# Shifting the SBUF tiles of a block-attention and two-MLP kernel to other byte addresses

## The chip, the cores and the metric

The kernel runs on one core of one Trainium2 chip. The metric is the device time of one execution in microseconds (us). The median of three runs of the kernel before is 985.55 us (985.31 to 985.72).

## The reference

The kernel computes an attention with a block-causal mask (blocks of 64 positions, 4 batches, 8 heads, 576 positions, head width 64) and feeds its 2,304 tokens of width 512 through two MLPs with a hidden width of 2,048. All arrays are float32.

```
scores = q @ k.T / sqrt(64); scores = where(block_i >= block_j, scores, -1e9)
x = softmax(scores) @ v                 # 2304 tokens x 512
h = x @ w1_in;  g = h * cos(h);         y = g @ w1_out
h = y @ w2_in;  g = max(h, 0) ** 2;   out = g @ w2_out
```

## The kernel before, in words

**Recording and order.** The body does not issue instructions at once: a `Recorder` notes every operation with its engine, its cost and what it reads and writes, a list scheduler (`schedule`) puts all operations in one order with its own cost figures, and `issue` emits them in that order. A tile gets its real buffer only when its first operation is emitted (`VTile.alloc`). The order doesn't depend on addresses.

**Precision.** Each float32 operand of the MLPs is split in a high and a low part (`hi_part`, `lo_part`), held as `fp32r`, and each product becomes three matmuls (`mm3`, all issued at L548): high by high and high by low with the same stationary operand, low by high with another. For every two matmuls that read a high operand on the split side there is thus one that reads the low part.

**The work by time.** Some 400 us are attention, mixed with the first halves of both products of the first MLP: `h_banks` multiplies the weights `w` (stationary, 128x128) by the tokens `xs1` or `xs2` (moving, 256 or 320 columns), `out_T` multiplies `w` (stationary) by the activations `g` (moving, 256 or 320 columns). What is left of the MLPs comes in three stages of five rounds (`ROUNDS`). In each, `quad` or `two` multiply weight parts `w` (stationary) by token parts `x0` to `x6` (moving, 256 columns) into `h` banks, and a second product makes `y`: in the first stage `out_T` with 512 moving columns of `g` (256 in the short round), in the second `g` stationary and `w` moving with 512 columns, in the third `out_quad`, `g` stationary and `w` moving with 256 columns. There the moving parts lie in buffers of several tags: two in `raw`, two in `x`, one in `so`, nine in `w` (`right_factors`), and the stationary ones in `ws`, `t`, `c`, `n`, `t0` to `t3` and the `g` tiles (`g_forms`).

**Memory.** A pool allocates its tiles one behind the other, and each takes a multiple of 32 bytes of every partition. Pools on the left are stacked upwards in the order in which they are opened: `const`, `wa` (16 weight tiles of 4,096 bytes), `cv` (`raw`, `t`, `c`), `st` (`so`, `ws`), `g`, `o`, then `xs1` and `tmp1`, in whose place `tmp3` opens later. Those on the right are stacked downwards: `att`, in whose place `wo` (7 weight tiles) and then `x3` (`x`, `x0` to `x6`) open later. `transition` (L607) closes the old pools and opens the new ones. Every large tile is a multiple of 128 bytes, but for `raw` (1,026 words, 4,128 bytes with padding), so that all tiles of a pool share one residue. Worked out from the declarations, and the first weight tile begins at byte 2,272:

| tiles | byte address modulo 128, before |
|---|---|
| `w` in `wa` and in `wo` | 96 |
| `raw`, first and second buffer | 96 and 0 |
| `t`, `c`, `so`, `ws`, `g`, `o`, `xs1`, `xs2`, tiles of `tmp1` and `tmp3` | 32 |
| `x`, `x0` to `x6`, and all large tiles of attention | 96 |
| `ident` and `zeros` | 0 and 64 |

Slices that the matmuls read start at multiples of 128 bytes within their tile, so an operand has its tile's residue.

**Warm-up.** At the start TensorE multiplies a tile `zeros` (bf16, 256 columns) by itself 40 times (kind "warm"), between the first transposes.

Of the kernel before, what the change touches and what calls it, by code (L numbers as in the profile page):

```python
# [10 lines left out]
F32 = mybir.dt.float32  # L11
F32R = mybir.dt.float32r
BF16 = mybir.dt.bfloat16
I32 = mybir.dt.int32
# [16 lines left out]
RAWS = 2  # L31
# [345 lines left out]
def real(v):  # L377
    return v.ap() if isinstance(v, View) else v
# [3 lines left out]
def kernel(  # L382
# [28 lines left out]
    def of(kind):  # L411
        def wrap(fn):
            def run(*args, **kw):
                with R.of(kind):
                    return fn(*args, **kw)

            return run

        return wrap
# [4 lines left out]
    def act(out, in_, func, bias=None, scale=None, accum_out=None, after=()):  # L424
        kw = {}
        n = sum(x is not None and not isinstance(x, float) for x in (bias, scale))
        if accum_out is not None:
            n += 1
        cost = out.size / 1.2 + (50 if psum(in_) else 92) + 93 * n + (49 if out.size == 512 and func == ACTF.Relu and bias is not None else 0) + (115 if out.halves != 3 else 0)

        def fn():
            kw = {a: real(x) for a, x in (("bias", bias), ("scale", scale), ("accum_out", accum_out)) if x is not None}
            return nc.scalar.activation(real(out), real(in_), func, **kw)  # L433

        return R.op("ACT", cost, fn, [x for x in (out, accum_out) if x is not None], [in_, bias, scale], after)
# [10 lines left out]
    def stt(out, a, s, b, op0, op1):  # L446
        dve(
            out.size / 0.96 + 68,
            lambda: nc.vector.scalar_tensor_tensor(real(out), real(a), s, real(b), op0=op0, op1=op1),  # L449
            [out], [a, b], int(not psum(a) and not psum(b)),  # L450
        )
# [5 lines left out]
    def flexible(kind, alts, w, r):  # L457
        R.any([alts[e] for e in FREE[kind].split()], w, r)
# [112 lines left out]
    def dma(out, in_, size, service=None):  # L571
        R.op(
            "DMA", max(400.0, size / 360.0), lambda: nc.sync.dma_start(out=real(out), in_=real(in_)), [out], [in_],
            lat=1250,
        ).service = size / 420.0 if service is None else service
# [20 lines left out]
    def opened(stack, *names, **kw):  # L596
        got = []
        for n in names:
            p = Pool(n, **kw)
            p.open(stack)  # L600
            got.append(p)
        return got

    def later(names, **kw):
        return [Pool(n, **kw) for n in names]

    def transition(closes, stack, opens, old):  # L607

        def fn():
            closes()  # L610
            for p in opens:
                p.open(stack if p.stack is None else p.stack)

        users = {o for o in R.ops if any(t.pool in old for t in o.tiles)}
        o = R.op("HOST", 0.0, fn, after=users)
        for p in opens:
            p.after = (o,)
        return o

    s1, att = ExitStack(), ExitStack()  # L620
    (dram,) = opened(ctx, "dram", space=DRAM)
    const, wa_p, cv, st_p, g_p, o_p = opened(ctx, "const", "wa", "cv", "st", "g", "o")
    (psum_p,) = opened(ctx, "ps", space=PSUM)
    banks = Banks(8, *BANKS)
    xs_p, tmp = opened(s1, "xs1", "tmp1")
# [2 lines left out]
    def T(pool, shape, dtype, tag, bufs=1):  # L628
        return R.tile(pool, shape, dtype, tag, bufs, whole=pool.kw.get("space") == PSUM)
# [68 lines left out]
    @of("weights")  # L698
    def weight_part(src, hi, lo):

        w = weight_piece(src)
        hi_part(hi, w)
        lo_part(lo, w, hi)

    @of("weights")
    def weight_piece(src, gate=()):

        w = T(cv, [128, 512], F32, "c", 3)
        if not wide:
            dma(w, src, 128 * 2048)  # L710
        else:


            raw = T(cv, [128, 1026], I32, "raw", RAWS)
            R.op(
                "DMA", 128 * 4096 / 360.0,
                lambda: nc.sync.dma_start(out=real(raw).bitcast(U8)[:, 1:4097], in_=src.bitcast(U8)), [raw], after=gate, lat=1250,
            ).service = 2400.0
            mid = View(raw, [lambda a: a[:, 1:1025].rearrange("p (n t) -> p n t", t=2)[:, :, 0]], np.arange(512), 3)
            top = View(  # L720
                raw, [lambda a: a[:, 2:1026].bitcast(I8).rearrange("p (n t) -> p n t", t=8)[:, :, 0]],
                np.arange(512), 3,
            )
            t = T(cv, [128, 512], I32, "t", 2)


            wi = w.bitcast(I32)
            act(t, top, ACTF.Relu, bias=minus56, scale=2.0**27)
            act(wi, top, ACTF.Relu, bias=minus56, scale=-2.0**27)
            flexible(  # L730
                "wt",
                {
                    "DVE": (
                        "DVE", 512 / 0.96 + 68,
                        lambda: nc.vector.tensor_tensor(real(wi), real(t), real(wi), op=ALU.subtract), 1,  # L735
                    ),
                    "POOL": (
                        "POOL", 512 * 2.1 + 350,
                        lambda: nc.gpsimd.tensor_tensor(real(wi), real(t), real(wi), op=ALU.subtract), 1,
                    ),  # L740
                },
                [w], [t, w],
            )
            stt(wi, mid, 5, wi, ALU.logical_shift_right, ALU.bitwise_or)
        return w
# [64 lines left out]
    @of("later")  # L810
    def left_weights(w, c, to):

        gate = R.ops[-1:]
        for k in range(2):
            left_parts([weight_piece(w[i * 128:i * 128 + 128, c * 512:c * 512 + 512], gate) for i in (k, k + 2)], k, to)

    @of("later")
    def right_weights(w, c, to):

        gate = R.ops[-1:]  # L820
        for m in range(2):
            rows = [c * 512 + i * 128 for i in (m, m + 2)]
            right_parts_of([weight_piece(w[r:r + 128, :], gate) for r in rows], m, to)
# [388 lines left out]
    def new_g():  # L1212
        return [[T(g_p, [128, 2, 512], F32R, f"g{i}{m}") for m in range(HALF // 2)] for i in "hl"]
# [4 lines left out]
    def first_in(b, r):  # L1218
        g = new_g()
        in_cos(tmp, w1i, xs[b, r], g, GROUPS[r - 1][1], TOGETHER if (b, r) == (0, 1) else 1)  # L1220
        return g
# [31 lines left out]
    for group, steps in WORK:  # L1253
        R.phase = 0 if group == (0, 1) else 1 + group[0]
        g = first_in(*group)
        if group == (0, 1):
            w1o = weights(wa_p, row_chunks(w1_out, 0, 2))
        for i in steps:
            attend(i)
        if group in ((0, 2), (1, 1)):  # L1260
            c = group[0]
            left_weights(w1_in, 2 + c, wi_d[c])
        if group in ((1, 2), (2, 1)):
            c = group[0] - 1
            staged_weights(row_chunks(w1_out, 2 + c, 3 + c), wo_d[c:c + 1])
        if group == (3, 1):
            wo_p, x3_p = later(("wo", "x3"), side="right")
            transition(att.close, ctx, [wo_p, x3_p], (sb,)).hook = lambda: banks.own.update(s=0, t=0, a=0, y=2)
        if group == (3, 2):
            (tmp3,) = later(("tmp3",))  # L1270
            transition(s1.close, ctx, [tmp3], (xs_p, tmp))
            left = factors(wi_d[:2], 0)
        first_out(*group, g)
# [149 lines left out]
    def g_forms():  # L1423

        small = [(st_p, f"ws{i}", 1) for i in range(2)] + [(cv, "t", 2)] * 2 + [(cv, "c", 3)] * 3
        small += [(tmp3, "n", 1)] + [(tmp3, f"t{i}", 1) for i in range(4)]
        large = [(g_p, f"g{i}{m}", 1) for i in "hl" for m in range(HALF // 2)]
        got = [{}, {}]
        for c in range(2):
            for i in (0, 3, 4, 5, 6, 1, 2):  # L1430
                if small:
                    got[c][i] = [T(pool, [128, 2, 256], F32R, tag, n) for pool, tag, n in (small.pop(0), small.pop(0))]
                else:
                    pool, tag, n = large.pop(0)
                    t = T(pool, [128, 2, 2, 256], F32R, tag, n)
                    got[c][i] = [t[:, j] for j in range(2)]
        return got
# [86 lines left out]
    for stage in range(3):  # L1524
# [4 lines left out]
        for turn_, i in enumerate(ROUNDS[stage]):  # L1529
# [3 lines left out]
            if stage < 2:  # L1533
                xs = (load_quarters if i < 4 else load_plain)(src, c0, xp_d[i] if stage and turn_ < 4 else None)
                g = new_g()
            else:
                if turn_:
                    xs = kept_parts(xp_d[i], FIRST if i < 4 else (0, 1, 4))
                g = g_forms()
# [90 lines left out]
```

## Time and profile before

| | |
|---|---|
| median of three runs | 985.55 us |
| the profiled execution's own time | 983.81 us |
| its span, first to last instruction | 981.9 us |
| mean granted clock of TensorE | 0.997 |
| busy: PE, weight loads, DVE, ACT, POOL | 960.9, 866.3, 714.6, 602.0, 208.2 us |
| moved by DMA | 185.29 MB, 189 GB/s |

PE is TensorE's matmul side, PEld its weight loads, which overlap matmuls. The end of a matmul in the profile is modelled and lies past the start of the next one, so the mean duration of a matmul says little: what one costs in a dense row is read from start to start. The chain of waits does this: it goes back from the last instruction to what released each step, and a piece "0.98 PE h x9" says that nine matmuls took 0.98 us from the first one's start to the next piece.

### The profile page before, as it was taken

To read this page: it belongs to the slowest core of one execution; us is meant where nothing else is said; L and a number is where in the kernel's file an instruction comes from. 1 tells how busy PE (TensorE), PEld (TensorE's weight loads), DVE (VectorE), ACT (ScalarE), POOL (GpSimd) and SP (SyncE) were. 2 spreads that over 40 slices of the span, in tenths; PEclk is the share of its full clock that TensorE was granted. 3 is DMA by queue.
4 is the path that set the end of the run, shared out by engine and by line. 5 is a ranking of instruction groups with operands and counts; after the bars stand their busy time and mean duration, and the time that the engine had idled before them with its cause. 6 is when DMAs were issued, how large, how long until landed. Compare 5 with 4: busy or idle time off the path is not lost.

```text
span 981.9 us, 19283 instructions
## 1 busy us (share of the span) xinstructions
PE 960.9 (98%) x6996; PEld 866.3 (88%) x6996; DVE 714.6 (73%) x1581; ACT 602.0 (61%) x1285; POOL 208.2 (21%) x313
## 2 busy tenths in 40 slices
PE   7879999999999999999999999999999999999998
PEld 5657987888898989999989889998898999999998
DVE  6898677685877455696878887978785747749565
ACT  6787578786987774483858476758574433324222
POOL 3563234455787780000000000000000000000000
PEclk9999999999999999999999999999999999999999
DMA  7754132455566256643266899796947679525321
GB/s 192 194 151 124 48 99 74 103 169 170 176 201 190 88 169 256 244 176 107 87 193 193 326 359 321 264 345 205 343 139 235 239 259 401 198 88 194 100 68 59
DMA packets 155150, 185.29 MB, mean 189 GB/s; under 512 B 71728, under 2 KB 119856, under 8 KB 155056
## 3 DMA queue, kind: packets, MB, share of 16 engines
q1 hardware_dynamic: 155056, 184.07, 57.1%
q8 instruction: 55, 0.90, 0.4%
q14 instruction: 39, 0.32, 0.1%
HBM read 114.29 MB, written 69.73 MB: 187 GB/s over the span
## 4 chain that ended last, share of the span: by engine, by line
PE 87%; DMA 5%; DVE 4%; ACT 1%; POOL 1%; issue 1%; SPq 0%; DVEq 0%; POOLq 0%
PE y L548 37%; PE h L548 35%; PE t L566 6%; PE a L558 5%; PE s L558 4%; PE s L548 1%; DMA x<-xp_d 1%; DMA w<-wf_d 1%; DMA wi_d<-so 1%; DMA x<-x_d 1%; DVE e L1033 1%; DMA xp_d<-x 1%; DMA w<-wi_d 1%; DVE c L735 1%; DVE c L449 1%
## 5 line engine op out<-in xcount | busy, mean ns | idle before, releaser
L548 PE MATMUL h<-x,w 128*128 128x256 f32 x2304 | 326.3, 283 | 0.9 <-DMA x<-xp_d 0.5
L548 PEld LDWEIGHTS h<-x,w 128*128 128x128 f32 x2304 | 304.5, 191 | 5.4 <-DVE r L442 1.1
L548 PE MATMUL y<-gh,w 128*128 128x256 f32 (+2 forms) x832 | 215.9, 330 | 6.9 <-POOL w L467 6.6
L548 PEld LDWEIGHTS y<-gh,w 128*128 128x128 f32 x832 | 144.6, 189 | 19.0 <-POOL w L467 7.6
L548 PE MATMUL y<-gl,w 128*128 128x256 f32 (+2 forms) x416 | 135.4, 329 | 0.0
L548 PE MATMUL y<-w,gh 128*128 128x512 f32 (+1 forms) x450 | 124.2, 355 | 0.5 <-DVE gh L490 0.4
L548 PEld LDWEIGHTS y<-w,gh 128*128 128x128 f32 x450 | 79.3, 189 | 12.6 <-DVE gh L490 0.6
L433 ACT ACTIVATE e<-e,st 128x256 f32<-128x256 f32 (+4 forms) x144 | 82.8, 577 | 9.2 <-DVE st L1033 7.7
L1033 DVE CUSTOM_DVE_ANT_0 e<-s,mask 128x128 f32<-128x128 f32 (+4 forms) x160 | 71.3, 478 | 22.4 <-PE s L558 14.8
L531 POOL TENSOR_SCALAR e<-e,st 128x256 f32<-128x256 f32 (+4 forms) x116 | 72.7, 637 | 62.8 <-DVE st L1054 36.7
L548 PEld LDWEIGHTS y<-gl,w 128*128 128x128 f32 x416 | 78.6, 189 | 6.5 <-issue 0.8
L548 PE MATMUL y<-w,gl 128*128 128x256 f32 (+1 forms) x306 | 83.7, 334 | 0.0
L472 ACT ACTIVATE gh<-r 128x512 fp32r<-128x512 f32 (+1 forms) x85 | 51.3, 610 | 38.9 <-DVE r L1391 17.2
L566 PE MATMUL t<-ident,e 128*128 128x128 f32 (+1 forms) x400 | 64.4, 280 | 4.6 <-DVE e L535 2.1
L442 DVE TENSOR_TENSOR o<-y,o 128x512 f32<-128x512 f32 (+1 forms) x55 | 34.9, 636 | 44.4 <-PE y L548 43.6
L490 DVE TENSOR_TENSOR gl<-r,gh 128x512 fp32r<-128x512 f32 (+1 forms) x83 | 54.7, 664 | 16.4 <-ACT gh L472 13.6
L548 PE MATMUL h<-xs2h,w 128*128 128x320 f32 x256 | 62.0, 313 | 0.0
L566 PEld LDWEIGHTS t<-ident,e 128*128 128x128 f32 (+1 forms) x400 | 46.1, 141 | 13.3 <-POOL e L531 4.4
L501 ACT ACTIVATE r<-t 128x384 f32<-128x384 f32 (+1 forms) x95 | 49.0, 531 | 13.4 <-PE t L566 11.7
L433 ACT ACTIVATE t<-raw,minus 128x512 int32<-128x512 int8 x64 | 48.7, 760 | 13.8 <-DMA raw<-in_moe_w_out_dram 8.1
L548 PEld LDWEIGHTS y<-w,gl 128*128 128x128 f32 x306 | 50.4, 188 | 6.1
L548 PE MATMUL h<-xs1h,w 128*128 128x256 f32 x256 | 53.3, 289 | 1.8 <-POOL w L467 0.8
(172 smaller groups left out, 1835.5 us busy)
## 6 DMA issues: line engine op xcount, KB each, us to landing
wi_d<-so SPq DMA_DIRECT2D x84, 256.0 KB, 2.8
w<-wi_d SPq DMA_DIRECT2D x42, 512.0 KB, 6.7
raw<-in_moe_w_in_dram SPq DMA_DIRECT2D x32, 512.0 KB, 4.6
raw<-in_moe_w_out_dram SPq DMA_DIRECT2D x32, 512.0 KB, 4.2
xp_d<-x SPq DMA_DIRECT2D x24, 512.0 KB, 6.1
x<-xp_d SPq DMA_DIRECT2D x24, 512.0 KB, 5.5
y_d<-o SPq DMA_DIRECT2D x34, 256.0 KB, 2.4
o<-y_d SPq DMA_DIRECT2D x32, 256.0 KB, 4.0
```

Of the source, the lines that this page charges most:

```text
L433: return nc.scalar.activation(real(out), real(in_), func, **kw)
L442: out.size / 0.96 + 68, lambda: nc.vector.tensor_tensor(real(out), real(a), real(b), op=op), [out], [a, b],
L449: lambda: nc.vector.scalar_tensor_tensor(real(out), real(a), s, real(b), op0=op0, op1=op1),
L472: "ACT": ("ACT", n / 1.2 + 92, lambda: nc.scalar.activation(real(hi), real(x), ACTF.Copy)),
L490: lambda: nc.vector.tensor_tensor(real(lo), real(x), real(f(hi)), op=ALU.subtract), 1,
L501: "ACT": ("ACT", n / 1.2 + 50, lambda: nc.scalar.activation(real(out), real(ps), ACTF.Copy)),
L531: lambda: nc.gpsimd.tensor_scalar(real(out), real(x), real(s), 1.0, op0=ALU.mult, op1=ALU.mult),
L548: lambda: nc.tensor.matmul(real(ps), lhsT=real(lhsT), rhs=real(rhs), start=start, stop=stop, skip_group_check=True),
L558: nc.tensor.matmul(real(ps), lhsT=real(l), rhs=real(r), start=start, stop=stop, skip_group_check=True)
L566: lambda: nc.tensor.transpose(real(out), real(in_), real(ident)[0:rows, 0:rows]), [out], [in_, ident],
L735: lambda: nc.vector.tensor_tensor(real(wi), real(t), real(wi), op=ALU.subtract), 1,
L1033: lambda: nc.vector.tensor_tensor_reduce(out=real(e), in0=real(ps), in1=real(m), scale=-1.0, scalar=BIG, op0=ALU.add, op1=ALU.min, accum_o ...
```

## The change

Small tiles that nothing reads or writes (`shim1` to `shim4`) are put between pools, and `raw` grows from 1,026 to 1,056 words, of which the same 1,026 are used. No operation is added, removed or moved.

```diff
+    def shim(stack, name, n, **kw):
+
+        if n:
+            p = stack.enter_context(tc.tile_pool(name=name, bufs=1, **kw))
+            p.tile([128, n // 4], F32, tag=name, name=name)
+
     def transition(closes, stack, opens, old):
 
         def fn():
             closes()
-            for p in opens:
+            for i, p in enumerate(opens):
+                if i:
+                    shim(stack, "shim4", 64, side="right")
                 p.open(stack if p.stack is None else p.stack)
@@
-    const, wa_p, cv, st_p, g_p, o_p = opened(ctx, "const", "wa", "cv", "st", "g", "o")
+    (const,) = opened(ctx, "const")
+    shim(ctx, "shim1", 32)
+    (wa_p,) = opened(ctx, "wa")
+    shim(ctx, "shim2", 64)
+    cv, st_p, g_p, o_p = opened(ctx, "cv", "st", "g", "o")
+    shim(ctx, "shim3", 96, side="right")
@@
-            raw = T(cv, [128, 1026], I32, "raw", RAWS)
+            raw = T(cv, [128, 1056], I32, "raw", RAWS)
```

Worked out in the same way, the residues become these; the last two columns name the moving and the stationary operand's.

| product | before: moving, stationary | after: moving, stationary |
|---|---|---|
| `h` from `xs1`, `xs2` by `w` | 32, 96 | 64, 0 |
| `h` from `x0` to `x6` by `w` | 96, 96 | 64, 0 |
| `y` from `g` by `w` (first MLP) | 32, 96 | 64, 0 |
| `y` from `w` by `g` (second MLP, second stage) | 96, 32 | 0, 64 |
| `y`, third stage, `w` moving (9 of 14 parts) | 96, 32 | 0, 64 |
| `y`, third stage, `raw` and `x` moving (4 of 14) | 96 (one `raw`: 0), 32 | 64, 64 |
| `y`, third stage, `so` moving (1 of 14) | 32, 32 | 64, 64 |
| attention, among themselves | 96, 96 | 0, 0 |

## Rows read from the trace of the kernel before

**Rows 1.** The page, busy time by engine over the whole span.

```profile
PE 960.9 (98%) x6996; PEld 866.3 (88%) x6996; DVE 714.6 (73%) x1581; ACT 602.0 (61%) x1285; POOL 208.2 (21%) x313
```

**Rows 2.** Busy time by stretch: stretch, length, engines, granted clock, DMA share, GB/s.

```profile
core 0: us, PE busy (x) PEld busy (x) DVE busy (x) ACT busy (x) POOL busy (x), PEclk, DMA share, GB/s
0.00:100.00 100.00, 83.96 (x582) 62.77 (x584) 79.70 (x210) 75.58 (x184) 47.73 (x73) 0.97 0.63 165
...
500.00:600.00 100.00, 99.92 (x597) 88.41 (x596) 83.27 (x155) 67.62 (x127) 0.00 (x0) 1.00 0.82 286
600.00:700.00 100.00, 100.00 (x657) 91.12 (x656) 84.40 (x152) 65.64 (x119) 0.00 (x0) 1.00 0.82 292
```

**Rows 3.** The page, the chain that ended last, by engine and by line.

```profile
PE 87%; DMA 5%; DVE 4%; ACT 1%; POOL 1%; issue 1%; SPq 0%; DVEq 0%; POOLq 0%
PE y L548 37%; PE h L548 35%; PE t L566 6%; PE a L558 5%; PE s L558 4%; PE s L548 1%; DMA x<-xp_d 1%; DMA w<-wf_d 1%; DMA wi_d<-so 1%; DMA x<-x_d 1%; DVE e L1033 1%; DMA xp_d<-x 1%; DMA w<-wi_d 1%; DVE c L735 1%; DVE c L449 1%
```

**Rows 4.** The chain in order of time: start, us to the next piece, matmuls.

```profile
108.44 7.04 PE h L548 x48
...
271.56 7.46 PE h L548 x64
...
492.69 20.54 PE y L548 x88
...
843.93 11.52 PE h L548 x96
...
862.67 6.60 PE y L548 x56
```

**Rows 5.** Groups of MLP matmuls on PE, shapes apart: count, busy us, mean ns.

```profile
L548 PE MATMUL h<-x,w 128*128 128x256 f32 x2304 | 326.3, 283 | 0.9 <-DMA x<-xp_d 0.5 <-DVE r L442 0.4
L548 PE MATMUL y<-w,gh 128*128 128x512 f32 x288 | 92.0, 395 | 0.0
L548 PE MATMUL y<-gh,w 128*128 128x512 f32 x256 | 83.3, 396 | 0.0
L548 PE MATMUL y<-gh,w 128*128 128x256 f32 x320 | 70.7, 292 | 6.9 <-POOL w L467 6.6 <-DVE w L490 0.2
L548 PE MATMUL h<-xs2h,w 128*128 128x320 f32 x256 | 62.0, 313 | 0.0
L548 PE MATMUL y<-gh,w 128*128 128x320 f32 x256 | 61.9, 312 | 0.0
L548 PE MATMUL h<-xs1h,w 128*128 128x256 f32 x256 | 53.3, 289 | 1.8 <-POOL w L467 0.8 <-POOL xs1h L467 0.6 <-DVE w L490 0.3
```

**Rows 6.** The chain inside 4.66 to 5.55 us, the bf16 warm-up matmuls.

```profile
4.64 0.98 PE h L548 x9
```

**Rows 7.** PE in order of time near the end: start, us, instruction, count.

```profile
974.96 0.84 PE L548 MATMUL y<-w,t 128*128 128x256 f32 x6
975.64 0.84 PE L548 MATMUL y<-w,gl 128*128 128x256 f32 x6
```

**Rows 8.** PE in order of time, third stage, moving operand in the second `raw` buffer.

```profile
816.95 0.88 PE L548 MATMUL y<-raw,gh 128*128 128x256 f32 x6
817.66 0.88 PE L548 MATMUL y<-raw,ws 128*128 128x256 f32 x6
```

**Rows 9.** Two groups on DVE that differ in width alone.

```profile
L442 DVE TENSOR_TENSOR r<-h,p 128x512 f32<-128x512 f32 x48 | 33.0, 688 | 30.1 <-PE h L548 29.7 <-ACT gh L472 0.3
L442 DVE TENSOR_TENSOR r<-h,r 128x320 f32<-128x320 f32 x32 | 15.5, 489 | 8.1 <-ACT r L433 8.0
```

**Rows 10.** The chain in order of time, entry of the third stage.

```profile
802.10 6.00 DMA w<-wi_d
...
808.16 9.17 DMA w<-wf_d
...
817.40 10.54 DMA x<-xp_d
```

## The prediction

> **What bounds the kernel now.** I read the page's busy times first: TensorE's matmul side is busy for 98% of the span, the next engine, DVE, for 73% [rows 1]. The stretches show where that is not the whole story: in the first 100 us PE is busy for only 84 us, from 500 to 700 us for all of it, with DVE at 83 and 84 us of 100 and the DMA share at 0.82; the granted clock is 1.00 there, the upper level of 2.4 GHz [rows 2]. The chain that ended last runs 87% over PE, and 37 + 35 = 72% of the span, 707 us, over the MLP matmuls of L548 [rows 3]. So what one dense MLP matmul costs, start to start, decides.
>
> The chain in order of time gives that cost by width and by the residues of the two operands. 256 columns, moving and stationary operand both at 96: 11.52 us / 96 = 120.0 ns. 256 columns, 64 bytes apart: 6.60 / 56 = 117.9 ns in the third stage (nearly all pairs there), 7.46 / 64 = 116.6 ns from `xs1`. 320 columns, 64 apart: 7.04 / 48 = 146.7 ns. 512 columns, 64 apart: 20.54 / 88 = 233.4 ns [rows 4]. At 2.4 GHz and a column a cycle they would be 106.7, 133.3 and 213.3 ns: every one is 9 to 13% above, and the surplus grows with the width (10 to 13, 13, 20 ns).
>
> The counts: 2,304 matmuls `h<-x,w`. 512 columns: 288 + 256 with the high part and half as many with the low part, 816. 320 columns: (256 + 256) x 1.5 = 768. 256 columns in the first stretch and in the first stage's short round: 256 x 1.5 = 384 from `xs1` and 320 x 1.5 = 480 from `gh` [rows 5]; in the third stage, by the code, four rounds of 7 x 2 x 12 = 168 and one of 84, 756. At the prices above the five kinds are 2,304 x 120.0 = 276 us, 816 x 233.4 = 190, 768 x 146.7 = 113, 1,236 x 117.9 = 146 and 384 x 116.6 = 45, 770 us in all. The chain holds 707 of these, 92%.
>
> **What the change does, part by part.** No instruction, wait or DMA is added, removed or moved. The shims hold bytes and no work, and the wider `raw` changes the distance of its two buffers and not what is moved. These cost nothing. What can change is the price of an access.
>
> The engines other than PE: two DVE groups that differ in width alone took 688 and 489 ns, 199 ns for 192 elements, 1.04 ns an element [rows 9], which is DVE's 0.96 GHz at one element a cycle, although these tiles lie 32 bytes off a multiple of 64. I take zero for DVE and, by the same reading, for ACT and POOL. For DMA no row shows an aligned and an unaligned transfer of the same kind; DMA holds 5% of the chain [rows 3], so a tenth faster or slower would be 5 us to either side, and I take zero, since the bytes and packets stay the same.
>
> The matmuls: here the rows say more. In one run the cost locks at (975.64 - 974.96) / 6 = 113.3 ns [rows 7]. 113.3 ns is 272 cycles, 256 + 16: one cycle for every 16 columns, that is for every 64 bytes of an fp32 row. The common 120.0 ns is 288 cycles, 256 + 32. So I read two terms: a **stream term** of one cycle for each 64 bytes, and a **collision term** of up to 16 more for the weight load that runs beside the matmul, 16 at equal residues (120.0) and some 11 on average at 64 bytes apart (117.9). A weight load reads 512 bytes of a partition: eight pieces of 64, which off a multiple of 64 touch two 64-byte lines each, 16 touches. Aligned they touch eight lines, and with the operands 64 bytes apart the two sides start on opposite halves of 128.
>
> That gives the collision term its bounds: gone altogether, or, if it knows nothing of alignment, only the step from 120.0 to 117.9 for the `h` matmuls from `x0` to `x6`, which move from equal residues to 64 apart. I take it as gone, because the locked run shows that 64 apart can cost none at all. For the stream term the nearest rows disagree. The bf16 matmuls, whose operands both lie on a multiple of 64, take 0.98 / 9 = 109 ns for 256 columns [rows 6], so without it 109 is possible; but they read half the bytes. The fp32 matmuls from the second `raw` buffer, the only ones whose moving operand begins on a multiple of 128, take (817.66 - 816.95) / 6 = 118 ns [rows 8], no less than their neighbours. An aligned stream beside an unaligned weight load thus gains nothing, and I leave the stream term in.
>
> The Trainium skill, TensorE: Matmul & The Clock Gate, section "Wait — 56ns, not 53.3ns?", gives a warm matmul as its columns at 2.4 GHz plus about 2.5 ns, whatever lies where. Rows 6 agree with it; the fp32 rows are 7 to 18 ns above it, so by that rule there is a surplus to win, and the sum would be that of the first rival.
>
> The sum with the collision term gone, other widths by the same 17/16 (estimates from the locked run: 141.7 and 226.7 ns): 2,304 x (120.0 - 113.3) = 15.4 us; 1,236 x (117.9 - 113.3) = 5.7; 384 x (116.6 - 113.3) = 1.3; 816 x (233.4 - 226.7) = 5.5; 768 x (146.7 - 141.7) = 3.8. Together 31.7 us of PE time. Against it, in the third stage the parts in `raw` and `x` go from 64 apart to equal residues: 4 of 14, 216 matmuls; at 2.1 ns each 0.5 us, which I neglect.
>
> Of this not all arrives. At most the chain's 92% does. At least what lies behind the attention: the MLP matmuls of the first 400 us are 113 + 45 + 480 x 117.9 = 57, so 215 us or 28% of 770, and there DVE, ACT and POOL take turns in ending waits; 92 - 28 = 64%. Late next is DVE at 84 us of 100 and the DMA queue: on entry to the third stage the chain runs 26 us over three loads, `w`, `w` and `x` [rows 10], and a faster PE only waits longer there. I take 80%: 31.7 x 0.8 = 25 us. The profiled execution's own time of 983.8 us, its span of 981.9 and 1.9 around it, becomes 958.4; the median of the runs stands 1.7 us above that execution, so **960 us**. Its own range is 956 to 965 (92% to 64%).
>
> **The rivals.**
> - *The stream term goes too.* Then the widths cost 109 ns and, with the same 2.3 ns over the columns, 135.6 and 215.6: 25.3 + 11.0 + 2.9 + 8.5 + 14.5 = 62 us, 80% of it 50, hence 936 us (928 to 946 by the two shares). For it: one cycle per 64 bytes is what a 64-byte piece that straddles two lines would cost, and every fp32 stream but one straddles. Against it: rows 8.
> - *Only the distance counts.* The 2,304 matmuls go from 120.0 to 117.9: 4.8 us, 92% of it 4.5, hence 981. For it: no fp32 row shows any gain from alignment itself.
> - *It does nothing.* Then 985.5. The step from 120.0 to 117.9 may come from the order of the matmuls and not from the residues, since the stages differ in both. The Trainium skill, TensorE: Matmul & The Clock Gate, section "Step-by-step: what each phase is for", speaks for this: TensorE has two independent read ports, and loading the next weights doesn't take bandwidth from the running matmul. Rows 4 speak against it as far as they show equal residues dearer.
> - *Slower.* With both operands on line boundaries the weight load and the stream start in step, and if they meet on the same line at every piece in spite of the 64 bytes, each matmul pays what equal residues pay now: 1,236 x 2.1 + 384 x 3.4 for 256 columns, and, by the same share of 1.8%, 816 x 4.2 + 768 x 2.6 = 9.3 us, 92% of it 8.6, hence 994. It decides from the point where a dense run outside `h<-x,w` costs more than 117.9 ns. For it: rows 8, where an aligned stream is not cheaper. Against it: 64 bytes apart is never the dearer distance in the rows.
>
> **How the numbers follow.** The forecast gets 0.34, the stream term gone too 0.25, distance alone 0.21, nothing 0.09, slower 0.11. A measurement of this kernel can tell about 0.2%, 2 us, from no change. The first three are faster by more than that, 0.80; same 0.09; slower 0.11. The range leaves out the last two and takes in the first three with their bounds: from 932, within the stronger rival, to 984, just above the 981 of distance alone.
>
> **What would show it.** Right: dense runs of `h<-x,w` near 113 ns instead of 120, the 512-column runs near 227, the 320-column ones near 142, and DVE, ACT and DMA durations unchanged; the span shorter mostly after 400 us; more waits of PE on DVE and on the loads of the third stage. The stream term is wrong if the 256-column runs fall to about 109; the collision term is wrong if they stay at 118 or above; the share that arrives is wrong if PE's runs shorten as said and the span doesn't follow by four fifths.

## The result and the profile after

| | before | after |
|---|---|---|
| median of four runs each | 985.43 us | **974.81 us** |
| the profiled execution's own time | 983.81 us | 974.84 us |
| its span | 981.9 us | 973.0 us |
| mean granted clock | 0.997 | 0.994 |

The ratio is 0.9893 [0.9876, 0.9911]: 10.6 us or 1.1% faster. 960 us was forecast, so the sign was right and the size 2.4 times too large (25 us against 10.6); 974.8 lies in the range of 932 to 984.

The page of the changed kernel, busy time by engine, and the chain that ended last by engine and by line:

```profile
PE 951.8 (98%) x6996; PEld 856.1 (88%) x6996; DVE 713.8 (73%) x1581; ACT 602.3 (62%) x1285; POOL 208.3 (21%) x313
...
PE 88%; DMA 5%; DVE 3%; ACT 2%; issue 1%; POOL 1%; SPq 0%; ACTq 0%; POOLq 0%; DVEq 0%
PE y L548 37%; PE h L548 34%; PE t L566 6%; PE a L558 5%; PE s L558 4%; DMA wi_d<-so 2%; PE s L548 1%; DMA x<-xp_d 1%; DMA w<-wf_d 1%; DMA x<-x_d 1%; DVE e L1046 1%; POOL e L531 0%; DVE c L449 0%; DVE c L748 0%; DVE so L490 0%
```

Beside [rows 1] PE has lost 9.1 us; DVE, ACT and POOL stand within 0.8 us of where they were, as forecast. The chain's shares [rows 3] hardly move. Busy time by stretch of the changed kernel (stretch, length, engines, granted clock, DMA share, GB/s):

```profile
core 0: us, PE busy (x) PEld busy (x) DVE busy (x) ACT busy (x) POOL busy (x), PEclk, DMA share, GB/s
0.00:100.00 100.00, 84.97 (x572) 63.02 (x573) 79.41 (x209) 75.92 (x184) 47.61 (x73) 0.95 0.62 162
500.00:600.00 100.00, 98.98 (x610) 88.03 (x609) 83.53 (x155) 67.45 (x127) 0.00 (x0) 1.00 0.83 290
600.00:700.00 100.00, 100.00 (x656) 90.39 (x655) 86.94 (x156) 68.28 (x124) 0.00 (x0) 1.00 0.84 297
```

The first 100 us gained nothing: 572 matmuls started there against 582 in [rows 2], at a granted clock of 0.95 against 0.97. The time was won later. In the stretch from 400 to 800 us 2,613 matmuls started against 2,549 before.

What one matmul costs shows where. The chain of the changed kernel in order of time (start, us to the next piece, matmuls), beside [rows 4]:

```profile
109.93 7.04 PE h L548 x48
...
273.00 7.74 PE h L548 x64
...
445.00 9.07 PE h L548 x80
457.48 12.82 PE y L548 x56
...
728.96 19.36 PE y L548 x83
...
802.64 8.72 DMA w<-wf_d
811.42 10.21 DMA x<-xp_d
...
837.59 10.88 PE h L548 x96
855.63 6.55 PE y L548 x56
```

Three pieces of the kernel before's chain, to be read beside the third, fourth and fifth of these:

```profile
444.44 9.59 PE h L548 x80
...
457.61 13.07 PE y L548 x56
...
734.38 19.37 PE y L548 x83
```

The third stage's `h` matmuls now take 10.88 / 96 = **113.3 ns instead of 120.0**; the first stage's run of 80 takes 9.07 / 80 = 113.4 ns instead of 9.59 / 80 = 119.9. All else moved little or not at all: 320 columns 7.04 / 48 = 146.7 as before, 512 columns in the first stage 12.82 / 56 = 228.9 instead of 13.07 / 56 = 233.4, in the second stage 19.36 / 83 = 233.3 as before, the third stage's `y` 6.55 / 56 = 117.0 instead of 117.9. And the `xs1` run near 272 us became dearer, 7.74 / 64 = 120.9 instead of 116.6.

The same over all dense MLP matmuls, from each one's start to the next one's start (steps with a pause in them left out), mean ns, and the gain as the difference times the count:

| kind (count) | before | after | gain, us | forecast, us |
|---|---|---|---|---|
| `h` from `x0` to `x6`, 256 (2,304) | 119.56 | 114.98 | 10.6 | 15.4 |
| `h` from `xs1`, 256 (384) | 116.67 | 117.49 | -0.3 | 1.3 |
| `y` by `out_T`, 256 (480) | 117.68 | 117.01 | 0.3 | } 5.7 |
| `y`, third stage, 256 (756) | 117.77 | 117.34 | 0.3 | } |
| 320 columns (768) | 146.65 | 146.6 | 0.0 | 3.8 |
| `y`, 512, first stage (384) | 232.07 | 229.35 | 1.0 | } 5.5 |
| `y`, 512, second stage (432) | 233.40 | 233.00 | 0.2 | } |
| **sum**, means times counts | 768.4 us | 756.2 us | **12.1** | 31.7 |

### The profile page after: what moved, and what is told of

Its sections match the earlier page's. It is cut to its first block, busy times and chain, and to the rows that moved or that the text cites. A ratio compares the mean times of both kernels' runs of the same rounds, so it can differ in the third digit from the quotient of the medians.

```text
span 973.0 us, 19283 instructions
## 1 busy us (share of the span) xinstructions
PE 951.8 (98%) x6996; PEld 856.1 (88%) x6996; DVE 713.8 (73%) x1581; ACT 602.3 (62%) x1285; POOL 208.3 (21%) x313
## 4 chain that ended last, share of the span: by engine, by line
PE 88%; DMA 5%; DVE 3%; ACT 2%; issue 1%; POOL 1%; SPq 0%; ACTq 0%; POOLq 0%; DVEq 0%
PE y L548 37%; PE h L548 34%; PE t L566 6%; PE a L558 5%; PE s L558 4%; DMA wi_d<-so 2%; PE s L548 1%; DMA x<-xp_d 1%; DMA w<-wf_d 1%; DMA x<-x_d 1%; DVE e L1046 1%; POOL e L531 0%; DVE c L449 0%; DVE c L748 0%; DVE so L490 0%
## 5 line engine op out<-in xcount | busy, mean ns | idle before, releaser
L548 PE MATMUL h<-x,w 128*128 128x256 f32 x2304 | 315.8, 278 | 1.7 <-DVE r L442 0.9
L548 PEld LDWEIGHTS h<-x,w 128*128 128x128 f32 x2304 | 294.4, 188 | 6.5 <-DVE r L442 1.7
L548 PE MATMUL y<-gh,w 128*128 128x256 f32 (+2 forms) x832 | 214.7, 329 | 7.3 <-POOL w L467 6.6
L548 PEld LDWEIGHTS y<-gh,w 128*128 128x128 f32 x832 | 144.3, 189 | 19.0 <-POOL w L467 7.6
L548 PE MATMUL y<-gl,w 128*128 128x256 f32 (+2 forms) x416 | 135.0, 328 | 0.0
L548 PE MATMUL y<-w,gh 128*128 128x512 f32 (+1 forms) x450 | 124.0, 354 | 0.4 <-DVE gh L490 0.4
L548 PEld LDWEIGHTS y<-w,gh 128*128 128x128 f32 x450 | 78.9, 188 | 12.6 <-DVE gh L490 0.6
L548 PEld LDWEIGHTS y<-gl,w 128*128 128x128 f32 x416 | 78.5, 189 | 6.2 <-issue 0.8
L548 PE MATMUL y<-w,gl 128*128 128x256 f32 (+1 forms) x306 | 83.5, 333 | 0.0
L548 PE MATMUL h<-xs2h,w 128*128 128x320 f32 x256 | 62.0, 313 | 0.0
L548 PEld LDWEIGHTS y<-w,gl 128*128 128x128 f32 x306 | 50.2, 188 | 6.1
L548 PE MATMUL h<-xs1h,w 128*128 128x256 f32 x256 | 53.5, 290 | 1.2 <-POOL w L467 0.7
```

What stands on the lines that cost most here:

```text
L548: lambda: nc.tensor.matmul(real(ps), lhsT=real(lhsT), rhs=real(rhs), start=start, stop=stop, skip_group_check=True),
```

## The experiments

One number explains most of what follows, so it is given for each kernel: the distance, moving minus stationary operand, of the 2,304 `h` matmuls, worked out from the declarations modulo 256 bytes. Before it is 0. After it is +64 for weights in `wa` and -64 for those in `wo`, since the seven tiles of 4,096 bytes and the shims leave the two pools 128 apart. "Low" is the share of these matmuls that take 115 ns or less, and the dense sum is made as in the table above, from each kernel's own means.

| kernel | distance of `h` | mean ns | low | dense sum, us | ratio to before |
|---|---|---|---|---|---|
| before | 0 | 119.6 | 0.01 | 768.4 | |
| after | +64 / -64 | 115.0 | 0.66 | 756.2 | 0.9893 [0.9876, 0.9911] |
| distance only | -64 | 115.8 | 0.48 | 758.7 | 0.9915 [0.989, 0.994] |
| aligned, equal | 128 / 0 | 118.7 | 0.14 | 765.0 | 0.9964 [0.995, 0.9978] |
| quarter apart | +32 / -96 | 117.4 | 0.18 | 762.4 | 0.9939 [0.9916, 0.9961] |
| all unaligned | +64 / -64 | 114.9 | 0.68 | 756.3 | 0.9905 [0.9891, 0.992] |
| -64 throughout | -64 | 115.7 | 0.49 | 758.4 | 0.9906 [0.9892, 0.992] |
| by width | +64 | 117.4 | 0.13 | 761.7 | 0.9931 [0.9917, 0.9944] |
| +64 throughout | +64 | 117.6 | 0.09 | 763.0 | 0.9936 [0.9923, 0.9949] |

**1. The distance alone.** The kernel before with one spare tile of 64 bytes ahead of `x3`, and nothing else; nothing is aligned, and `raw` is as it was.

```diff
-            for p in opens:
+            for i, p in enumerate(opens):
+                if i:
+                    gap = stack.enter_context(tc.tile_pool(name="shim4", bufs=1, side="right"))
+                    gap.tile([128, 16], F32, tag="shim4", name="shim4")
                 p.open(stack if p.stack is None else p.stack)
```

> The kernel before, with one spare tile of 64 bytes in front of the token parts of the last three stages, and nothing else: their residue goes from 96 to 32, the weights stay at 96. So h from x0 to x6 has its operands 64 bytes apart, and both stay 32 bytes off a multiple of 64. Theory 'distance': what the change gained there comes from the distance alone; the dense runs of h<-x,w fall from 120 to about 115 ns as in the changed kernel, and the time is near its 975 us. Theory 'alignment': a weight load that begins on a multiple of 64 touches half as many lines, and that was the gain; the runs stay at 118 to 120 ns and the time at 983 to 985 us.

Measured 976.66 us against 984.7. The chain in order of time, first and third stage:

```profile
444.08 9.42 PE h L548 x80
457.03 12.83 PE y L548 x56
...
839.38 10.91 PE h L548 x96
857.44 6.54 PE y L548 x56
```

One shim of 64 bytes brings the third stage's run from 120.0 to 10.91 / 96 = 113.6 ns and the first stage's from 119.9 to 9.42 / 80 = 117.8. So most of the gain is distance, and its price is more than the 2.1 ns that [rows 4] suggested.

**2. Everything aligned, the distance left out.** The changed kernel without its fourth shim.

```diff
-                    shim(stack, "shim4", 64, side="right")
+                    shim(stack, "shim4", 0, side="right")
```

> The changed kernel without its fourth spare tile: weights and token parts of the last three stages all begin on a multiple of 128, so they are aligned and have equal residues (0 and 0). Theory 'distance': the dense runs of h<-x,w are back at 120 ns and the time is 984 to 987 us. Theory 'alignment': they stay near 115 ns and the time near 975 us.

Measured 981.59 us. The same run in its chain:

```profile
842.80 11.42 PE h L548 x96
```

119.0 ns. With the distance of 64 left out 0.4% is left of the 1.1%. Of the 3.4 us that the dense sum loses here `h` gives 2,304 x (119.56 - 118.7) = 2.0. Told apart by their order, its matmuls with weights in `wa`, at a distance of 128, take 118.6 ns and those in `wo`, at 0, take 118.8, so the distance of 128 is not all of it; where the rest comes from was not shown.

**3. A quarter of 128 apart.**

```diff
-                    shim(stack, "shim4", 64, side="right")
+                    shim(stack, "shim4", 96, side="right")
```

> The changed kernel with the fourth spare tile of 96 bytes instead of 64: the weights of the last three stages begin on a multiple of 128, their token parts 32 bytes past one. Theory 'distance': 32 bytes apart lies between equal (120 ns) and 64 apart (115 ns), so 117 to 119 ns and 979 to 984 us. Theory 'alignment': the weight load is still aligned, the stream is not; if the weight load's alignment is what counts, 115 ns and 975 us.

Measured 979.14 us, `h` at 117.4 ns in the mean: between equal and 64 apart.

**4. A grid of residues.** Nothing but dense fp32r matmuls with the pattern of L548, moving and stationary operand at each of 16 pairs of residues modulo 128, in three widths and after two kinds of pause. Attention and MLPs are left out, so its time of 539.47 us compares with nothing.

```diff
+        L = {0: "a", 32: "b", 64: "c", 96: "d"}
+        for m in L:
+            for s in L:
+                run(f"n256{L[m]}{L[s]}x", 256, m, s, 36)
```

> Only matmuls: the attention and the MLPs are left out and the output is zeros. Runs of 36 fp32 matmuls of 256 columns, and of 24 of 512 and of 320 columns, three for each pair as in the kernel, for all 16 pairs of residues 0, 32, 64, 96 of the moving and the stationary operand, each pair once straight behind the run before and once behind a pause; then 256 columns at offsets of 4, 8, 16 and 20 bytes. Theory 'distance': the cost depends on the difference of the residues alone: at 256 columns 120 ns for equal ones, less for the others, 113 to 115 ns at 64 apart, whichever of the two is aligned. Theory 'alignment': the pairs with a stationary operand at 0 or 64 are the cheap ones. Theory 'phase': the same pair costs 113 or 118 to 120 ns by how the run begins, so the two runs of a pair differ.

Its chain in order of time, all of a run's matmuls a piece (the last step of a piece leads into the next run):

```profile
32.94 4.24 PE n256acx L59 x36
...
58.48 4.09 PE n256cax L59 x36
...
403.90 3.51 PE n320cax L59 x24
...
506.67 4.38 PE n256m4s0z L59 x36
```

The two letters are the residues of the moving and the stationary operand, a to d for 0, 32, 64 and 96. The prices below leave out the first steps of a run, in which it settles. 320 columns took 146.4 to 146.9 ns at all 16 pairs: none of these layouts touches them. 512 columns took 228.8 at (0, 64) and (32, 96) and 233.3 at (64, 0) and (96, 32), with nothing to tell aligned pairs from the others. 256 columns took 118.5 to 118.8 at equal residues and 117.8 at three of the four pairs that are 64 apart; at the pair that the change makes, (64, 0), they took 113.3. The weights' base was 128 modulo 256 here, so that this pair is -64 in the count above: hence the next grid goes modulo 256.

The same kernel ends with starts that are no multiple of 32. With the stationary operand at 0 and the moving one 4 bytes past 0, 256 columns took 122.1 ns (`m4s0`), 8 bytes past it 120.7 and 16 bytes past it 119.0; with the moving operand at 20 and the stationary one at 116 they took 123.3. The stationary operand 4, 8 or 16 bytes off, beside a moving one at 64, gave 118.3 to 118.9. So a moving operand 4 bytes off costs more than any pair of multiples of 32 in the grid.

**5. The same modulo 256, after four kinds of run.** The letters a to h stand for residues 0, 32, ... 224, of the moving and then of the stationary operand; the last letter is the kind of run before (a: 320 columns, b: 512, c: a narrow weight load, d: equal residues). Narrow weight loads (64 and 32 columns) are added. Attention and MLPs are left out again.

```diff
+        D = [(m, s) for m in (0, 64, 128, 192) for s in (0, 64, 128, 192)]
+        D += [(32, s) for s in (32, 96, 160, 224)] + [(m, 32) for m in (96, 160, 224)]
+        for e in range(4):
+            for m, s in D:
...
+                go(f"n256{tag(m, s)}{A[e]}", 256, m, s, 24)
```

> Only matmuls again: attention and MLPs are left out, the output is zeros. Runs of 24 fp32 matmuls of 256 columns, with the weights in the order of the kernel's products, for moving and stationary operands at 0, 64, 128 and 192 modulo 256 and for some pairs 32 bytes off these; each pair entered in four ways (behind 320 columns, behind 512, behind a narrow weight load, behind equal residues). Then 512 columns in two entries, and weight loads of 64 and of 32 columns in place of 128. Theory 'distance and phase': equal residues modulo 128 never reach 113 ns; 64 apart is at 113.3 or at 117.8 by how the run is entered, aligned or not; which side the 64 bytes lie on shows at 512 columns (229 against 233 ns). Theory 'alignment': 113.3 ns comes with a stationary operand on a multiple of 64 or 128 alone, whatever the entry. Stream and collision terms: with a weight load of 32 columns the collisions are a quarter, so 256 columns cost 113 to 115 ns at every pair if the stream term of one cycle for each 64 bytes is there whatever the residues, and 107 to 109 at aligned pairs if it comes from straddled lines.

Its chain in order of time, 24 matmuls of 256 columns a piece (the last step of a piece leads into the next run; within a run 2.72 to 2.75 us stands for 113.3 ns, 2.82 to 2.84 for 117.8, 2.86 to 2.88 for 120.0):

```profile
25.00 2.87 PE n256aaa L82 x24
28.32 2.74 PE n256aca L82 x24
...
38.05 2.83 PE n256caa L82 x24
41.31 2.86 PE n256cca L82 x24
...
80.50 2.83 PE n256bda L82 x24
...
160.23 2.74 PE n256bdb L82 x24
...
257.90 2.83 PE n256acd L82 x24
...
339.19 3.50 PE n512aca L82 x15
...
350.95 3.46 PE n512caa L82 x15
354.84 3.41 PE n512cca L82 x15
...
401.65 3.49 PE n512bda L82 x15
...
517.91 1.78 PE n256bdcols64q L82 x15
519.70 1.72 PE n256bbcols64q L82 x15
...
538.76 1.72 PE n256aacols32q L82 x15
540.48 1.70 PE n256cacols32q L82 x15
...
543.89 1.71 PE n256bdcols32q L82 x15
545.61 1.70 PE n256bbcols32q L82 x15
```

What is to be seen, with all its runs counted start to start, once they have settled:
- Distance 0 costs 119.4 to 120.2 ns in all 20 runs, 128 costs 118.3 to 120.1.
- At a distance of 64 the same matmuls have **two prices, 113.3 or 117.8 ns**, and keep one for the whole run. Which one depends on what ran before: `aca` is low and `acd` high, `bdb` low and `bda` high. At -64 16 of 24 runs were low, at +64 3 of 24. The low price needs no alignment: (0, 64) and (32, 96) were low in three of four each. Of all pairs at -64 the aligned ones were low in 12 of 16 runs and those 32 bytes off in 4 of 8.
- 512 columns go the other way: 226.7 at distance 0 in most runs, 229 at +64 in 11 of 12, 233.3 at -64, 232 to 233 at 128.
- With a weight load of 32 columns beside them, 256 columns take 113.3 at every pair, `aa`, `ca`, `ac`, `bd`, `bb`. At this width 113.3 is thus what stays when the load is small, and it does not fall below 113.3 where all is aligned. What lies above it goes with the load; but the run with the small load also writes 32 rows of output instead of 128, and the two were not told apart. A load of 64 columns costs nothing at distance 0 (`bb`) and some 6 ns at -64 (`bd`), the reverse of the full load. 512 columns stay at 229 to 233 ns with either narrow load, so what their surplus is made of remains open.

**6, 7, 11. Repeats.** The changed kernel twice more, the distance-only kernel once more.

> The changed kernel itself, to be compared with the next run on one chip. Theory 'distance': 974 to 976 us, within 0.2% of the next run. Theory 'alignment as well': 2 us or more under the next run.

> The kernel before with 64 bytes in front of the token parts of the last three stages alone, once more, with five rounds. Theory 'distance': 975 to 977 us, as the changed kernel on the same chip. Theory 'alignment as well': 977 to 979 us.

> The changed kernel itself on the same chip as the run beside it: 0.987 to 0.990 of the kernel before.

The changed kernel gave 972.38 us against 986.02 (0.9869 [0.9855, 0.9884]) and 972.68 against 984.2 (0.9879 [0.9865, 0.9892]); distance only, on the same chip as the first of these, 975.96 (0.9903 [0.9886, 0.9919]). Distance alone thus brings 10.1 of 13.6 us, and what the changed kernel has beyond it, 3.6 us, is clear of the noise there: the two intervals don't meet. The dense costs repeat within 0.1 ns. In both repeats the stretch up to 100 us shows the clock of 0.97 that the kernel before had; this one is from the first repeat:

```profile
0.00:100.00 100.00, 83.77 (x576) 62.42 (x578) 80.01 (x210) 75.76 (x184) 47.60 (x73) 0.97 0.62 163
```

**8. Everything off alignment by 32 bytes, all distances kept.**

```diff
-    shim(ctx, "shim1", 32)
+    shim(ctx, "shim1", 64)
@@
-    shim(ctx, "shim3", 96, side="right")
+    shim(ctx, "shim3", 64, side="right")
```

> The changed kernel with everything moved up by 32 bytes (the first spare tile 64 bytes instead of 32, the third 64 instead of 96): every distance between the operands of the MLP products is that of the changed kernel, modulo 256 too, and no large tile begins on a multiple of 64 any more. Theory 'distance': 972 to 976 us, ratio to the kernel before 0.987 to 0.990, as the changed kernel. Theory 'alignment as well': the 2 to 4 us by which the changed kernel lay under the run with the distance alone are gone, 976 to 979 us, ratio 0.990 to 0.993.

Measured 975.15 us against 984.38. By its time this is the theory 'distance', by its ratio of 0.9905 the other one: its interval [0.9891, 0.992] meets those of distance only, of the changed kernel's first runs and, barely, of its second repeat, but not that of the first repeat, [0.9855, 0.9884]. The time alone does not decide. The dense costs do: 114.91 ns for `h` (114.98 with alignment), 756.3 us in all (756.2), and the third stage's run to the hundredth:

```profile
836.74 10.88 PE h L548 x96
```

So no part of the gain in the dense matmuls comes from alignment. What makes this span longer than that of the first repeat, 972.2 against 970.0 us, is waiting: from the first `h` of the three stages on, PE's pauses (what its steps with a pause in them take beyond the dense price) sum to 4.6 us here and to 2.7 there. They vary as much between executions of the changed kernel itself, 4.7 us in the first profile and 3.1 in the second repeat.

**9. -64 throughout.** All weights at 0, `x0` to `x6` and `xs1` at 192 modulo 256: by the grid the side that is low oftener.

```diff
+                if len(opens) > 1:
+                    shim(stack, f"shim{4 + i}", 64 if i else 128, side="right")
-                if i:
-                    shim(stack, "shim4", 64, side="right")
@@
+    shim(s1, "shim6", 128)
```

> The changed kernel with the distance turned the way that the matmul runs preferred: modulo 256 the token parts lie 64 bytes below the weights in all h products (weights at 0 in both pools, tokens at 192; in the changed kernel half of them were 64 above). In the matmul runs 64 below locked at 113.3 ns in 16 of 24 entries, 64 above in 3 of 24. Theory 'distance and phase': the mean of dense h<-x,w runs falls from 115.0 to about 114, those from xs1 from 117.5 to 115 to 116, 2 to 4 us less than the changed kernel: ratio 0.984 to 0.987, 969 to 972 us. Rival, that in the kernel the entry decides and not the side: no change against it, 972 to 975 us.

Measured 976.01 us: no better than the changed kernel. `h` costs what it costs in the distance-only kernel, which also has -64 throughout, 115.7 and 115.8 ns; `xs1` fell to 116.0 with 0.45 of its matmuls low.

```profile
445.00 9.42 PE h L548 x80
...
839.47 10.91 PE h L548 x96
```

Both runs repeat those of experiment 1 to the hundredth, although all addresses differ: as far as these two kernels go, the signed distance fixes them.

**10. A distance for each width.** `h` at +64, and for the second stage's 512 columns distance 0, where the grid has them cheapest.

```diff
+                if len(opens) > 1:
+                    shim(stack, f"shim{4 + i}", 192 if i else 128, side="right")
-                if i:
-                    shim(stack, "shim4", 64, side="right")
@@
+    shim(ctx, "shim6", 192)
+    (g_p,) = opened(ctx, "g")
+    shim(ctx, "shim7", 64)
+    (o_p,) = opened(ctx, "o")
```

> The changed kernel with the distances chosen by width, modulo 256: the token parts 64 above the weights in all h products of the last three stages (in the changed kernel's trace 64 above cost 114.5 ns and 64 below 115.2), and the g tiles level with the weights, because 512 columns cost 226.7 ns at distance 0 in the matmul runs and 233.3 at 64 below; 256-column products of g with w pay for it. Theory 'distance': second-stage y runs from 233.0 to about 227 ns (432 matmuls, 2.7 us), first-stage ones from 229.4 to 227 (1 us), h<-x,w to 114.4 (1.3 us), against it y of 256 columns from 117.0 to 120 (423 matmuls, 1.3 us) and part of the third stage (1 us): 2 to 3 us less than the changed kernel, ratio 0.985 to 0.988. Rival, that the costs of the matmul runs don't carry over because each run in the kernel is entered anew: no change at 512 columns, ratio 0.988 to 0.990. The alignment of both operands stays that of the changed kernel.

Measured 977.73 us. The 512 columns did what the grid says, 18.85 / 83 = 227.1 ns instead of 233.3, in the mean 228.3; `h` went the other way.

```profile
733.06 18.85 PE y L548 x83
...
840.38 11.31 PE h L548 x96
```

432 x (233.0 - 228.3) = 2.0 us won, 2,304 x (117.4 - 115.0) = 5.5 lost.

**12. +64 throughout**, that is experiment 10 without the two shims around `g`, so that `h` alone is asked about.

```diff
-    shim(ctx, "shim6", 192)
-    shim(ctx, "shim7", 64)
```

> The run before last without its step at the g tiles: modulo 256 the token parts lie 64 above the weights in all h products of the last three stages, and g stays 64 above the weights as in the changed kernel. It tells apart what took the 113 ns away from h<-x,w there (117.4 ns on average). Theory 'what runs before decides': it was the other g distance, so that the 512-column runs in between hand over another phase; here h<-x,w is at 114 to 115 ns and the time at 970 to 974 us, ratio 0.985 to 0.988. Rival 'the side decides': 64 above is the worse side in the kernel as in the matmul runs; h<-x,w stays near 117 ns and the time at 976 to 978 us.

Measured 978.76 us.

```profile
843.18 11.31 PE h L548 x96
```

117.8 ns, 0.09 of all low: it was +64 throughout, and not the tiles `g`, that cost experiment 10 its `h`. It still beats distance 0 by 1.9 ns. Yet +64 is not dear in itself: in the changed kernel, with the `h` matmuls told apart by their order, those at +64 (weights in `wa`) take 114.7 ns and those at -64 (in `wo`) 115.2. The same +64 is cheap where runs at -64 lie between and dear where there are none. That fits a price that goes with what ran before, as in experiment 5, but no run of the whole kernel isolates it.

## Why the prediction was right in sign and wrong in size

- **What bounds the kernel: right.** PE's dense matmuls decide: in the repeats the span fell from 981.9 to 970.0 and 970.2 us at the kernel before's clock, and the dense sum from 768.4 to 756.1 and 756.3.
- **The step that failed: the collision term "gone altogether".** The prediction let alignment remove it for every product. Alignment did nothing for the dense costs (experiment 8), and nearly every product but `h` from `x0` to `x6` was 64 apart before and stayed on the same side, +64 for `xs1` and `out_T`, -64 for `y` with `w` moving: together these 3,204 matmuls gained 1.6 us where 16.3 was forecast. The argument from the number of 64-byte lines that a load touches came out wrong, and no run shows such lines. [rows 7], read as "64 apart can cost none at all", showed one of two states at that distance; the kernel before had runs in both. That the sign was right is owed to the one step that the forecast shares with its rival, the distance of `h`.
- **The `h` term: right in kind, 10.6 us instead of 15.4.** Not all 2,304 reach 113.3 ns, only two thirds do.
- **The collision term as such: borne out for 256 columns.** There the surplus of up to 120.0 - 113.3 = 6.7 ns, 16 cycles, hangs on where the next weights lie beside the moving operand, and it is gone with a load of 32 columns (experiment 5, in which the output shrinks as well). For 512 columns it isn't: their 229 to 233 ns stay with small loads. The Trainium skill, TensorE: Matmul & The Clock Gate, section "Step-by-step: what each phase is for", says that loading the next weights takes no read bandwidth from the running matmul. These fp32r matmuls don't agree: beside a full load they took 113.3 to 120.0 ns by the distance alone.
- **The stream term stays: right for 256 columns**, and the rival that lets it go is refuted: with small loads 256 columns cost 113.3 ns aligned and unaligned alike. Its size at another width was wrong: 320 columns showed 146.7 at all 16 pairs of the grid, so the 141.7 at which the prediction put them free of collisions was seen nowhere.
- **The rival "only the distance counts": right in cause, too small in price.** It took 2.1 ns from [rows 4], a run in the dear one of the two states; measured over all `h` matmuls it was 3.8 ns for one shim and 4.6 for the change. Its 981 us lie 6 us above the 974.8 measured, the forecast's 960 lie 15 below.
- **The rivals "nothing" and "slower": refuted**, the second by 512 columns and by `y` in the third stage that became no dearer, although 4 of the 14 parts of the latter moved to equal residues (three from 64 apart and one from 32, where the prediction has all four from 64). Only `xs1` did, by 0.8 ns or 0.3 us.
- **The share that arrives, 80%: too low, if anything.** 10.6 us of 12.1 is 88%, and in the repeats 13.6 and 11.5 us stand against 768.4 - 756.1 = 12.3 and 12.1. It can't be had closer, since executions of one kernel differ by as much: the first profile's span is 973.0 us, the first repeat's 970.0, at dense sums that agree within 0.2. At the 600th matmul, behind the stretch with the lower clock, 0.8 us of these 3.0 are there (103.1 against 102.3 us); another 2.0 are PE's pauses from the first `h` of the three stages on, 4.7 against 2.7 us, where the kernel before has 2.9. The bound of 64% was a little low in itself: of the 480 matmuls that it puts into the first 400 us, 96 belong to the first stage's short round, 11 us or some 1.5 points. What was to be late next showed little: waits on DVE grew by half a microsecond. PE's waits in the changed kernel (what waits for what: us, times, longest):

```profile
PE y L548 <- POOL w L467: 6.6, 4, 4.0
...
PE h L548 <- DVE r L442: 0.9, 2, 0.6
```

  In [rows 5] these are 6.6 and 0.4 us. And on entry to the third stage the chain holds two loads of 8.72 + 10.21 = 18.9 us, where [rows 10] have three of 25.7 in all.
- **Zero for DVE, ACT, POOL and DMA: right** by the busy times above, for DMA as far as its share shows it (0.83 and 0.84 from 500 to 700 us, 0.82 before).

Open: why +64 and -64 by turns hold two thirds of the `h` matmuls at the low price, where -64 throughout holds half and +64 throughout a tenth. Whether the +64 or the -64 comes first within a round was not varied. Nor is it settled how all of the 3.6 us between the distance-only kernel and the changed one comes about; the dense sums account for 758.7 - 756.2 = 2.5, and PE's pauses vary by some 2 us from one execution to the next. No version beat the changed kernel.

## What to carry to other kernels

Before you align SBUF tiles, look at the distance between the moving and the stationary operand of the dense fp32 matmuls modulo 256 bytes: one spare tile of 64 bytes gave three quarters of what the whole change gave here, and the alignment gave the dense matmuls nothing. When a matmul's cost per run takes a few fixed values, as 113.3, 117.8 and 120.0 ns here, a run of rows shows one state and no price; count all runs of a kind before a difference enters a sum. A grid of operand addresses in a kernel of its own gives the prices, but which of them a kernel gets, only the kernel's own trace shows.

## What the runs showed of the hardware

- fp32r matmuls of 256 columns beside a full weight load cost 119.4 to 120.2 ns at distance 0 modulo 256 bytes, 118.3 to 120.1 at 128, and 113.3 or 117.8 at 64; 512 columns have nearly the opposite order (226.7 at 0, 233.3 at -64), and 320 columns have one price, 146.7, at all pairs tried.
- At a distance of 64 the price is a state that lasts through a run and goes with what ran before (experiment 5: 16 of 24 runs low at -64, 3 of 24 at +64, though both are as far apart).
- Moving every tile 32 bytes off the multiples of 64, at the same distances, changed no dense cost of the changed kernel by more than 0.4 ns (`h` 114.98 and 114.91). Below 32 bytes the start counts: a moving operand 4 bytes off took 122.1 ns for 256 columns.
